# Second stage of an attention and two-layer expert kernel in two passes of four units, with partial sums in DRAM

## Chip, cores and metric

The kernel runs on one core of a Trainium2 chip. The metric is the device time of one execution in microseconds (us); the time before is the median of three runs, 1608.3 us (1608.15 to 1608.68).

## What is computed

Three layers follow each other. The first is an attention over 32 memory slots; its result (4608 tokens of 512) goes through a gated layer of width 1536, and that through a layer of width 2048.

```python
a = softmax(phi, over the sequence)            # 8 batches, 8 heads, 576 x 32
k_m, v_m = a^T k, a^T v                        # 32 x 64 for each head
x = softmax(q k_m^T / 8) v_m                   # 4608 x 512
x = (silu(x w_gate) * (x w_val)) w_out         # width 1536
out = elu(x w_in) w_out2                       # width 2048
```

All weights come as float64 and are turned into float32 parts on the chip.

## The kernel before

The hidden layer of 1536 is cut into twelve **units** of 128 (NU1 = 12), two units to a **pair**; a batch has 576 tokens, worked in two **halves** of HS = 288 columns. Every float32 product is made of three matmuls on rounded parts (high by high, high by low, low by high), so a unit's gate and val take 6 matmuls each (`up1`, tiles pg and pv) and its share of the output 4 x 3 (`down`).

- **Attention weights.** Since v_m has only 32 rows for each head, `vw` (L133) multiplies it into the gate and val weights of a pair: 16 short matmuls (pvw), then ACT and VectorE make the two parts (L143, L144). A unit's gate and val are then products of a vw tile and the attention probabilities `at`.
- **Stage 1** runs over the 8 batches with units 0 to 3 (UA = 4). Beside the matmuls of batch b stand the attention tasks of batches b + 1 and b + 2 and conversions of weights, dealt out by `tick`. The sum of the four units goes to DRAM as p1 (`down1`, L373), and `at` does too.
- **Stage 2** runs over the batches again with units 4 to 11. `load2` brings `at` back (tile at2); `load_p1` brings the partial sum of a half into the p1 tile, of which there is one buffer (L453). `down2` runs two units late (LAG = 2); with the last unit of a half it adds the four accumulators to p1 (L475) and stores the half as x1 (L476).
- **Stage 3** takes x1 in nine blocks of 512 tokens through 16 units (`unit3`, `down3`; tiles pu, g, e).
- **Conversion** of a weight tile (`load_w`, L86): a 512 KB load of float64 (wr, four buffers) on SP; ACT (L100); four VectorE instructions on the tiles wv and wc (L101, L102, L104, L105), the last of which reads wr and frees it; then, for tiles that are split, ACT (L107) and two GpSimd instructions (L108, L109), else one (L111). There are 68: 24 of w1g (four to a pair), 12 of w1o, 32 of w2 (two halves to each of 16 units).
- **What sets the order.** A scheduler orders each engine's instructions; L98 keeps a conversion behind the last h traced before it. Engines and SP's queue run in that order, and an instruction that waits holds those behind it.

Before the change, w1g of pairs 4 and 5 and w1o 7 to 11 are converted in the last batch of stage 1 (L411 to L413); 19 halves of w2 follow in stage 2, one in most halves and eight in the last batch (L518), and 13 in stage 3, one per unit (L526, L583).

Of the kernel before, what the change touches and what calls it, by code (L numbers as in the profile page):

```python
# [8 lines left out]
F32 = mybir.dt.float32  # L9
# [9 lines left out]
B, H, S, D, M = 8, 8, 576, 64, 32  # L19
NT = B * S  # L20
DM, F1, F2 = 512, 1536, 2048
KD = DM // 128
HS = S // 2
# [3 lines left out]
UA = 4  # L27
NCH = 5
NWA = 24
NWB = 16  # L30
NWE = 14
NWC = 10
NKV = 5
NQ = 3

# [2 lines left out]
def attention_moe_moe(ctx: ExitStack, tc: tile.TileContext, qT, phiT, kv, kv4, w1g, w1o, w2, out):  # L38
    nc = tc.nc
# [30 lines left out]

    at_d = [dram.tile([128, 2, 2, S], F32R, name=f"atd{b}") for b in range(B)]
    p1_d = [dram.tile([128, KD, S], F32, name=f"p1d{b}") for b in range(B)]
    x1_d = [dram.tile([128, KD, S], F32, name=f"x1d{b}") for b in range(B)]

    last = {}
# [43 lines left out]
    def load_wg(p, k, pool):  # L119
        load_w(WG, p, k, w1g[p, k], pool, False)  # L120

    def load_wo(u, pool):
        load_w(WO, u, 0, w1o[u], pool)
# [9 lines left out]
    def vw(b, p, pools):  # L133
        t = VW[b, p] = vx_p.tile([128, 2, 2, 512], F32R, tag="vx", name="vw")
        ps = [pool.tile([128, 512], F32, tag=tag, name="pvw") for pool, tag in pools]

        def head(j, g):
            r, c = slice(64 * g, 64 * g + 64), slice(32 * j, 32 * j + 32)
            return mm(ps[g][c], lhsT=Bs[b].vt[r, j, :], rhs=WG[p][j][r], start=True, stop=True)  # L139

        together([lambda j=j, g=g: head(j, g) for j in reversed(range(KD)) for g in (1, 0)])
        for g in range(2):
            act(out=t[:, 0, g, :], in_=ps[g], func=AF.Copy)  # L143
            tt(out=t[:, 1, g, :], in0=ps[g], in1=t[:, 0, g, :].bitcast(F32), op=ALU.subtract)  # L144
# [10 lines left out]
    def down(ps, w, hs, ms, start, stop):  # L155
        mm(ps, lhsT=w[0][:, ms], rhs=hs[0], start=start, stop=False)  # L156
        mm(ps, lhsT=w[1][:, ms], rhs=hs[0], start=False, stop=False)  # L157
        mm(ps, lhsT=w[0][:, ms], rhs=hs[1], start=False, stop=stop)  # L158
# [224 lines left out]
    def load2(b):  # L383
        at2[b] = av_p.tile([128, 2, 2, S], F32R, tag="at", name="at2")
        nc.sync.dma_start(out=at2[b].bitcast(F32), in_=at_d[b].bitcast(F32))


    def wg_tasks(p):
        return [lambda k=k: load_wg(p, k, wa_p) for k in range(KD)]

    prev = None
    for b in range(B):
        todo = []
# [14 lines left out]
            fr += [lambda u=u: load_wo(u, wb_p) for u in (4, 5, 6)]  # L408
        if b == B - 1:
            fr.append(lambda: load2(0))  # L410
            fr += wg_tasks(4) + [lambda: load_wo(7, wb_p), lambda: vw(0, 2, V2), lambda: load_wo(8, wb_p)]  # L411
            fr += wg_tasks(5) + [lambda: load_wo(9, wb_p), lambda: vw(0, 3, V2), lambda: load_wo(10, wb_p),
                                 lambda: load_wo(11, wb_p)]  # L413
        for i in range(max(len(bk), len(fr))):
            todo += fr[i:i + 1] + bk[i:i + 1]
        if b + 1 < B:
# [41 lines left out]
    def more_w2(pool, n=1):  # L458
        for _ in range(n):
            load_w2(*todo2.pop(0), pool)  # L460

    def load_p1(b, hf):
        t = p1_p.tile([128, KD, HS], F32, tag="p1", name="p1l")
        nc.sync.dma_start(out=t, in_=p1_d[b][:, :, HS * hf:HS * hf + HS])
        return t

    def down2(q):
        b, hf, u, hs, accs, p1 = q
        if u == UA:
            accs += [ps_acc.tile([128, HS], F32, tag=f"acc{m}", name=f"acc{m}") for m in range(KD)]  # L470
        for m in range(KD):
            down(accs[m], WO[u][0], hs, slice(128 * m, 128 * m + 128), u == UA, u == NU1 - 1)
        if u == NU1 - 1:
            for m in range(KD):
                tt(out=p1[:, m, :], in0=accs[m], in1=p1[:, m, :], op=ALU.add)  # L475
            nc.sync.dma_start(out=x1_d[b][:, :, HS * hf:HS * hf + HS], in_=p1)  # L476

    def load3(j):
        xt = []
# [14 lines left out]

    LAG = 2
    pend = []
    for p in (4, 5):
        vw(0, p, V2)
    w2q = [wa_p] * 4 + [we_p] * 7 + [wa_p] * 8
    vwq = []  # L500
    for b in range(B):
        for hf in range(2):
            p1 = load_p1(b, hf)
            accs = []
            if hf == 0 and b + 1 < B:
                load2(b + 1)
            for u in range(UA, NU1):
                s = gate1(b, u, at2[b], HS * hf, True)
                pend.append((b, hf, u, val1(b, u, at2[b], HS * hf, s, True), accs, p1))
                if len(pend) > LAG:  # L510
                    down2(pend.pop(0))
                if vwq:
                    vw(*vwq.pop(0), V2)
                if hf == 1 and u % 2 == 1 and b + 1 < B:
                    vwq.append((b + 1, u // 2))
                elif hf == 1 and u == 7 and b == B - 1:
                    nxt = load3(0)
                if u % 2 == 1 if b == B - 1 else u == 8 and len(w2q) > 8:  # L518
                    more_w2(w2q.pop(0))
# [105 lines left out]
```

## Time and profile before

| | us |
|---|---|
| median of three runs | 1608.3 |
| profiled execution: time | 1609.44 |
| profiled execution: span | 1607.6 |
| TensorE (PE) busy | 1533.4 |
| VectorE (DVE) busy | 988.0 |
| ScalarE (ACT) busy | 654.0 |
| GpSimd (POOL) busy | 166.2 |

The span is the time between the first and the last instruction of the profiled execution; its device time is 1.8 us longer. PE is the matmul engine, PEld its weight load, SP the engine that issues DMA transfers. Stage 1 lasts to about 361 us, stage 2 to about 811 us. Idle time of an engine counts only where the end of the kernel waits for it, so the views that matter are those by stretches and by waits.

### The profile page before, as it was taken

How to read it: one execution, taken by the hardware profiler on the slowest of the kernel's cores; microseconds unless marked ns; L12 is line 12 of the kernel's file. 1: busy time of each engine (PE TensorE's matmuls, PEld its weight loads, DVE VectorE, ACT ScalarE, POOL GpSimd, SP SyncE). 2: the span in 40 equal slices, each digit the busy share in tenths (PEclk: the TensorE clock that was granted, in tenths of full speed). 3: DMA queues.
4: the chain of work that ended last, by engine and by line, in shares of the span. 5: the costliest groups of instructions: out<-in, count | busy, mean ns of one | idle time of the engine just before them, and what ended most of it. 6: DMA issues, size and time to landing. Idle time of an engine off the chain costs nothing.

```text
span 1607.6 us, 24193 instructions
## 1 busy us (share of the span) xinstructions
PE 1533.4 (95%) x9816; PEld 1311.5 (82%) x9816; DVE 988.0 (61%) x1702; ACT 654.0 (41%) x1249; POOL 166.2 (10%) x119
## 2 busy tenths in 40 slices
PE   3599999979999999999998999999999999999998
PEld 2478789769999999999976788888888888888887
DVE  7997876795444454435889755555555555555554
ACT  3455444543333333333544433334343434343333
POOL 1400010241101011000435100000000000000000
PEclk7799999999999999999999999999999999999999
DMA  8887332452322232211522101001010101010000
GB/s 346 293 307 265 109 112 75 170 192 72 106 77 82 73 102 86 73 60 45 157 85 74 53 1 45 9 6 48 1 53 0 53 0 53 1 53 1 27 1 27
DMA packets 62961, 136.32 MB, mean 85 GB/s; under 512 B 6528, under 2 KB 37248, under 8 KB 60800
## 3 DMA queue, kind: packets, MB, share of 16 engines
q1 hardware_dynamic: 53632, 125.32, 22.7%
q10 hardware_dynamic: 9216, 9.44, 1.7%
q8 instruction: 77, 1.26, 0.3%
q14 instruction: 36, 0.29, 0.1%
HBM read 96.99 MB, written 37.75 MB: 84 GB/s over the span
## 4 chain that ended last, share of the span: by engine, by line
PE 81%; DVE 14%; DMA 2%; issue 2%; ACT 1%; SPq 0%; POOL 0%; ACTq 0%; DVEq 0%; POOLq 0%
PE acc L565 7%; PE acc L564 7%; PE acc L566 7%; PE pu L538 7%; PE pu L539 7%; PE pu L540 7%; PE acc L156 4%; PE acc L157 4%; PE acc L158 4%; PE pg L151 3%; PE pv L151 3%; PE pv L153 3%; PE pg L153 3%; PE pv L152 3%; PE pg L152 3%; PE pvw L139 3%
## 5 line engine op out<-in xcount | busy, mean ns | idle before, releaser
L538 PE MATMUL pu<-x1s,whi 128*128 128x512 f32 x576 | 224.7, 390 | 2.5 <-DVE g L554 2.5
L564 PE MATMUL acc<-whi,hh 128*128 128x512 f32 x576 | 224.5, 390 | 2.1 <-ACT hh L162 2.1
L566 PE MATMUL acc<-whi,hl 128*128 128x512 f32 x576 | 222.4, 390 | 3.3 <-DVE hl L164 3.3
L540 PE MATMUL pu<-x1s,wlo 128*128 128x512 f32 x576 | 224.8, 390 | 0.0
L539 PE MATMUL pu<-x1s,whi 128*128 128x512 f32 x576 | 224.7, 390 | 0.0
L565 PE MATMUL acc<-wlo,hh 128*128 128x512 f32 x576 | 224.2, 389 | 0.0
L553 DVE SCALAR_TENSOR_TENSOR g<-e,g 128x512 f32<-128x512 f32 x144 | 107.5, 747 | 157.5 <-ACT g L552 157.5
L162 ACT ACTIVATE hh<-g 128x512 fp32r<-128x512 f32 x144 | 91.0, 632 | 216.9 <-DVE g L554 216.9
L551 ACT ACTIVATE e<-g 128x512 f32<-128x512 f32 x144 | 90.8, 631 | 210.0 <-DVE g L550 210.0
L183 DVE SCALAR_TENSOR_TENSOR h<-s,pv 128x288 f32<-128x288 f32 x192 | 86.5, 451 | 140.8 <-PE pv L153 118.6
L164 DVE TENSOR_TENSOR hl<-g,hh 128x512 fp32r<-128x512 f32 x144 | 99.9, 694 | 88.3 <-ACT hh L162 88.2
L156 PE MATMUL acc<-hh,whi 128*128 128x288 f32 x512 | 151.0, 296 | 0.0
L157 PE MATMUL acc<-hh,wlo 128*128 128x288 f32 x512 | 150.6, 294 | 0.0
L158 PE MATMUL acc<-hl,whi 128*128 128x288 f32 x512 | 149.4, 295 | 0.0
L162 ACT ACTIVATE hh<-h 128x288 fp32r<-128x288 f32 x192 | 85.1, 443 | 138.9 <-DVE h L183 137.2
L164 DVE TENSOR_TENSOR hl<-h,hh 128x288 fp32r<-128x288 f32 x192 | 97.0, 505 | 63.0 <-ACT hh L162 62.8
L550 DVE TENSOR_SCALAR g<-pu 128x512 f32<-128x512 f32 x144 | 99.1, 689 | 55.2 <-PE pu L540 51.8
L566 PEld LDWEIGHTS acc<-whi,hl 128*128 128x128 f32 x576 | 108.0, 188 | 28.4 <-DVE hl L164 6.1
L151 PE MATMUL pg<-at,vw 128*128 128x288 f32 x384 | 119.4, 311 | 10.4 <-DVE vw L144 6.0
L564 PEld LDWEIGHTS acc<-whi,hh 128*128 128x128 f32 x576 | 108.3, 188 | 25.4 <-ACT hh L162 3.0
L538 PEld LDWEIGHTS pu<-x1s,whi 128*128 128x128 f32 x576 | 108.3, 188 | 25.3 <-DVE g L554 2.9
L539 PEld LDWEIGHTS pu<-x1s,whi 128*128 128x128 f32 x576 | 108.5, 188 | 22.6
(87 smaller groups left out, 3187.9 us busy)
## 6 DMA issues: line engine op xcount, KB each, us to landing
kvr<-kv SPq DMA_DIRECT2D x32, 512.0 KB, 7.9
wr<-w SPq DMA_DIRECT2D x32, 512.0 KB, 3.6
wr<-w1g SPq DMA_DIRECT2D x24, 512.0 KB, 4.9
qr<-qT SPq DMA_DIRECT2D x16, 576.0 KB, 5.9
atd<-at SPq DMA_DIRECT2D x8, 1152.0 KB, 5.3
p1d<-p ACTq DMA_DIRECT2D x64, 144.0 KB, 2.0
p1l<-p1d SPq DMA_DIRECT2D x16, 576.0 KB, 4.1
at<-atd SPq DMA_DIRECT2D x8, 1152.0 KB, 5.2
```

What stands on the lines that cost most here:

```text
L151: mm(ps, lhsT=wh, rhs=ah, start=g == 0, stop=False)
L156: mm(ps, lhsT=w[0][:, ms], rhs=hs[0], start=start, stop=False)
L157: mm(ps, lhsT=w[1][:, ms], rhs=hs[0], start=False, stop=False)
L158: mm(ps, lhsT=w[0][:, ms], rhs=hs[1], start=False, stop=stop)
L162: act(out=hh, in_=h, func=AF.Copy)
L164: tt(out=hl, in0=h, in1=hh.bitcast(F32), op=ALU.subtract)
L538: mm(ps, lhsT=wh[:, k, :], rhs=xh, start=k == 0, stop=False)
L539: mm(ps, lhsT=wh[:, k, :], rhs=xl, start=False, stop=False)
L540: mm(ps, lhsT=wl[:, k, :], rhs=xh, start=False, stop=k == KD - 1)
L564: mm(accs[c], lhsT=hs[0][:, cs], rhs=wh, start=u == 0, stop=False)
L565: mm(accs[c], lhsT=hs[0][:, cs], rhs=wl_, start=False, stop=False)
L566: mm(accs[c], lhsT=hs[1][:, cs], rhs=wh, start=False, stop=u == NU2 - 1)
```

## The change

Stage 2 runs over the batches twice. The first pass takes units 4 to 7, adds p1 and stores the result in a new DRAM buffer p2; the second takes units 8 to 11, adds p2 and stores x1. Of the conversions in the last batch of stage 1 only w1o 7 stays. The others and 22 halves of w2 are queued in `conv`, of which stage 2 takes one in each half, and two in each half of the last batch of the second pass; ten halves of w2 are left for stage 3. The vw of pairs 4 and 5 are made when the second pass comes to them.

```diff
-NWB = 16
-NWE = 14
-NWC = 10
+NWB = 8
+NWE = 20
+NWC = 12
...
+    p2_d = [dram.tile([128, KD, S], F32, name=f"p2d{b}") for b in range(B)]
...
-            fr += wg_tasks(4) + [lambda: load_wo(7, wb_p), lambda: vw(0, 2, V2), lambda: load_wo(8, wb_p)]
-            fr += wg_tasks(5) + [lambda: load_wo(9, wb_p), lambda: vw(0, 3, V2), lambda: load_wo(10, wb_p),
-                                 lambda: load_wo(11, wb_p)]
+            fr += [lambda: load_wo(7, wb_p), lambda: vw(0, 2, V2), lambda: vw(0, 3, V2)]
...
     def down2(q):
-        b, hf, u, hs, accs, p1 = q
-        if u == UA:
+        b, hf, u, hs, accs, p1, dst = q
+        first, last_u = u % UA == 0, u % UA == UA - 1
+        if first:
...
-            nc.sync.dma_start(out=x1_d[b][:, :, HS * hf:HS * hf + HS], in_=p1)
+            nc.sync.dma_start(out=dst[b][:, :, HS * hf:HS * hf + HS], in_=p1)
...
-    for p in (4, 5):
-        vw(0, p, V2)
-    w2q = [wa_p] * 4 + [we_p] * 7 + [wa_p] * 8
+
+    conv = [lambda p=p, k=k: load_wg(p, k, wa_p) for p in (4, 5) for k in range(KD)] + \
+        [lambda u=u: load_wo(u, wa_p) for u in range(2 * UA, NU1)] + \
+        [lambda pool=pool: more_w2(pool) for pool in [we_p] * 10 + [wa_p] * 4 + [wb_p] * 4 + [wa_p] * 4]
     vwq = []
...
+    for ps, (src, dst) in enumerate(((p1_d, p2_d), (p2_d, x1_d))):
+        for b in range(B):
+            nb, np_ = (b + 1, ps) if b + 1 < B else (0, ps + 1)
+            for hf in range(2):
+                p1 = load_p1(b, hf, src)
+                accs = []
+                if hf == 0 and np_ < 2:
+                    load2(nb)
+                for u in range(UA * (ps + 1), UA * (ps + 2)):
...
+                    if hf == 1 and u % 2 == 1 and np_ < 2:
+                        vwq.append((nb, u // 2 + UA // 2 * (np_ - ps)))
+                    elif hf == 1 and u == 9 and np_ == 2:
+                        nxt = load3(0)
+                    if u % (2 if np_ == 2 else 4) == 1:
+                        conv.pop(0)()
...
-    w2q = [wb_p] * 8 + [wc_p] * 5
+    w2q = [wa_p] * 4 + [wc_p] * 6
```

Lines of the changed kernel lie one further up to L383 of before (L101 becomes L102, L183 L184); L475, L476 and L464 become L472, L473 and L460.

On **VectorE in the last batch of stage 1** there stood before, among others, these twelve instructions in a row (wc and wv are a conversion's, h and hl a unit's):

```order
L144 TENSOR_TENSOR vw<-pvw,vw 128x512
L105 SCALAR_TENSOR_TENSOR wc<-wr,wc 128x512
L104 TENSOR_SCALAR wc<-wv 128x512
L144 TENSOR_TENSOR vw<-pvw,vw 128x512
L183 SCALAR_TENSOR_TENSOR h<-s,pv 128x288
L105 SCALAR_TENSOR_TENSOR wc<-wr,wc 128x512
L164 TENSOR_TENSOR hl<-h,hh 128x288
L101 TENSOR_SCALAR wc<-wv 128x512
L183 SCALAR_TENSOR_TENSOR h<-s,pv 128x288
L102 SCALAR_TENSOR_TENSOR wv<-wv,wc 128x512
L101 TENSOR_SCALAR wc<-wv 128x512
L104 TENSOR_SCALAR wc<-wv 128x512
```

In the changed kernel this follows between the same two vw tiles:

```order
L145 TENSOR_TENSOR vw<-pvw,vw 128x512 x2
L184 SCALAR_TENSOR_TENSOR h<-s,pv 128x288
L165 TENSOR_TENSOR hl<-h,hh 128x288
L184 SCALAR_TENSOR_TENSOR h<-s,pv 128x288
L165 TENSOR_TENSOR hl<-h,hh 128x288
L145 TENSOR_TENSOR vw<-pvw,vw 128x512 x2
```

The conversions between the two vw and behind them are gone; what is left there are the h and hl of two units.

On **VectorE at the end of a half of stage 2** (here the first) the four adds stood before between the h and hl of the unit that comes after:

```order
L183 SCALAR_TENSOR_TENSOR h<-s,pv 128x288
L475 TENSOR_TENSOR p1l<-acc_4616,p1l 128x288
L475 TENSOR_TENSOR p1l<-acc_4617,p1l 128x288
L164 TENSOR_TENSOR hl<-h,hh 128x288
L475 TENSOR_TENSOR p1l<-acc_4618,p1l 128x288
L475 TENSOR_TENSOR p1l<-acc_4619,p1l 128x288
```

Now the steps of a conversion stand among them:

```order
L184 SCALAR_TENSOR_TENSOR h<-s,pv 128x288
L102 TENSOR_SCALAR wc<-wv 128x512
L472 TENSOR_TENSOR p1l<-acc_4461,p1l 128x288
L472 TENSOR_TENSOR p1l<-acc_4462,p1l 128x288
L103 SCALAR_TENSOR_TENSOR wv<-wv,wc 128x512
L165 TENSOR_TENSOR hl<-h,hh 128x288
L472 TENSOR_TENSOR p1l<-acc_4463,p1l 128x288
L472 TENSOR_TENSOR p1l<-acc_4464,p1l 128x288
L105 TENSOR_SCALAR wc<-wv 128x512
L184 SCALAR_TENSOR_TENSOR h<-s,pv 128x288
L106 SCALAR_TENSOR_TENSOR wc<-wr,wc 128x512
```

L102 of the conversion moved ahead of the adds, L103 between them, L105 and L106 behind; in all 30 halves that are not in the last batch of the second pass it reads so or nearly so.

On **SP in stage 2**, around the stores of batch 2, a raw weight load (wr) stood before behind the load of p1, and the load of p1 right behind the store that frees its buffer:

```order
L88 DMA wr<-w 128x1024
L476 DMA x1d_125<-p1l 512x1x288
L464 DMA p1l<-p1d_117 128x4x288
L88 DMA wr<-w 128x1024
L385 DMA at_6472<-atd_111 128x2304
L476 DMA x1d_125<-p1l 512x1x288
L464 DMA p1l<-p1d_118 128x4x288
```

Now a raw weight load stands between that store and the load of p1:

```order
L460 DMA p1l<-p1d_117 128x4x288
L473 DMA p2d_125<-p1l 512x1x288
L89 DMA wr<-w1o 128x1024
L460 DMA p1l<-p1d_117 128x4x288
L386 DMA at_5382<-atd_111 128x2304
L473 DMA p2d_125<-p1l 512x1x288
L89 DMA wr<-w1o 128x1024
L460 DMA p1l<-p1d_118 128x4x288
```

The load of the next batch's at2 (L386) now follows the p1 load of each first half; the store of a first half comes behind it.

## Rows read from the trace of the kernel before

**Rows 1.** the page, busy us of each engine, share of the span, instructions.
```profile
PE 1533.4 (95%) x9816; PEld 1311.5 (82%) x9816; DVE 988.0 (61%) x1702; ACT 654.0 (41%) x1249; POOL 166.2 (10%) x119
```

**Rows 2.** busy us by stretches (then granted clock, DMA share, GB/s), a stage 2 batch.
```profile
451.06:506.78 55.72, 55.72 (x457) 51.73 (x463) 26.21 (x56) 20.16 (x44) 6.29 (x4) 1.00 0.26 84
```

**Rows 3.** the same view, last batch of stage 1 into stage 2.
```profile
315.30:367.29 51.99, 42.86 (x313) 35.88 (x312) 50.11 (x74) 26.20 (x56) 25.04 (x18) 0.93 0.58 194
```

**Rows 4.** groups of TensorE there: count, busy us, mean ns, idle before and what ended it.
```profile
L156 PE MATMUL pd<-hh,whi 128*128 128x288 f32 x48 | 14.5, 304 | 1.7 <-DVE vw L144 1.2 <-DVE h L183 0.4
...
L151 PE MATMUL pg<-at,vw 128*128 128x288 f32 x18 | 6.3, 348 | 5.7 <-DVE vw L144 5.7
...
L139 PE MATMUL pvw<-wg,vt 64*32 64x512 f32 x64 | 5.8, 630 | 1.5 <-ACT p L377 1.4 <-DVE h L183 0.2
L151 PE MATMUL pv<-at,vw 128*128 128x288 f32 x17 | 5.7, 337 | 0.2 <-DVE h L183 0.2
```

**Rows 5.** TensorE in order of time there: start, us, idle before and what ended it.
```profile
361.24 0.61 PE L151 MATMUL pg<-at,vw 128*128 128x288 f32 x1 [3.47 <-DVE vw L144]
```

**Rows 6.** the chain that ended last, in order of time: start, us, what.
```profile
356.31 3.50 DMA wr<-w
...
360.50 0.70 DVE vw L144
```

**Rows 7.** VectorE in order of time, adds of a half within a conversion.
```profile
757.32 0.42 DVE L101 TENSOR_SCALAR wc<-wv 128x512 int32<-128x512 int32 x1
757.66 0.81 DVE L475 TENSOR_TENSOR p1l<-acc,p1l 128x288 f32<-128x288 f32 x2
758.39 0.68 DVE L102 SCALAR_TENSOR_TENSOR wv<-wv,wc 128x512 int32<-128x512 int32 x1
...
759.36 0.81 DVE L475 TENSOR_TENSOR p1l<-acc,p1l 128x288 f32<-128x288 f32 x2
...
760.79 1.70 DVE L105 SCALAR_TENSOR_TENSOR wc<-wr,wc 128x512 f32<-128x512 uint32 x1
```

**Rows 8.** next matmul on the accumulators, in order of time; then busy time by stretches.
```profile
760.59 0.29 PE L156 MATMUL acc<-hh,whi 128*128 128x288 f32 x1
...
760.00:780.00 20.00, 20.00 (x153) 20.00 (x152) 14.67 (x28) 8.56 (x20) 9.81 (x7) 1.00 0.42 139
```

**Rows 9.** SP's DMA issues in order of time, same place.
```profile
760.20 0.54 SPq L476 DMA_DIRECT2D x1d<-p1l  x1
762.57 0.33 SPq L88 DMA_DIRECT2D wr<-w  x1
763.50 0.54 SPq L464 DMA_DIRECT2D p1l<-p1d  x1
```

**Rows 10.** groups of TensorE from 830 to 900 us, head of stage 3.
```profile
L564 PE MATMUL acc<-whi,hh 128*128 128x512 f32 x50 | 19.7, 395 | 2.1 <-ACT hh L162 2.1
L566 PE MATMUL acc<-whi,hl 128*128 128x512 f32 x51 | 19.5, 405 | 3.3 <-DVE hl L164 3.3
```

**Rows 11.** p1 loads (L464) issued before 300 us, from 300 to 750, from 750.
```profile
DMA to landing us min/median/max: 8.8/8.8/8.8
...
DMA to landing us min/median/max: 4.0/4.1/4.2
...
DMA to landing us min/median/max: 5.2/5.7/6.1
```

**Rows 12.** stage 2 to 3: the chain that ended last, then TensorE in order of time.
```profile
811.19 3.30 DMA x1d<-p1l
...
819.52 0.50 PE L538 MATMUL pu<-x1s,whi 128*128 128x512 f32 x1 [2.47 <-DVE g L554]
```

**Rows 13.** busy time by stretches, 100 us of stage 3.
```profile
1010.00:1110.00 100.00, 100.00 (x443) 82.81 (x442) 54.99 (x82) 37.94 (x61) 0.00 (x0) 1.00 0.07 22
```

**Rows 14.** GpSimd in order of time, first step of two conversions in stage 3.
```profile
886.94 1.74 POOL L108 TENSOR_TENSOR wv<-wv,whi 128x512 f32<-128x512 f32 x1 [2.69 <-DVE wc L104]
...
893.08 1.73 POOL L108 TENSOR_TENSOR wv<-wv,whi 128x512 f32<-128x512 f32 x1 [2.70 <-DVE wc L104]
```

More of the change, by code (lines that the diff above doesn't have):

```diff
@@ L460, in more_w2, with load_p1 @@
             load_w2(*todo2.pop(0), pool)
-    def load_p1(b, hf):
+    def load_p1(b, hf, src):
         t = p1_p.tile([128, KD, HS], F32, tag="p1", name="p1l")
-        nc.sync.dma_start(out=t, in_=p1_d[b][:, :, HS * hf:HS * hf + HS])
+        nc.sync.dma_start(out=t, in_=src[b][:, :, HS * hf:HS * hf + HS])
         return t
     def down2(q):
-        b, hf, u, hs, accs, p1 = q
-        if u == UA:
+        b, hf, u, hs, accs, p1, dst = q
+        first, last_u = u % UA == 0, u % UA == UA - 1
+        if first:
             accs += [ps_acc.tile([128, HS], F32, tag=f"acc{m}", name=f"acc{m}") for m in range(KD)]
         for m in range(KD):
-            down(accs[m], WO[u][0], hs, slice(128 * m, 128 * m + 128), u == UA, u == NU1 - 1)
-        if u == NU1 - 1:
+            down(accs[m], WO[u][0], hs, slice(128 * m, 128 * m + 128), first, last_u)
+        if last_u:
             for m in range(KD):
                 tt(out=p1[:, m, :], in0=accs[m], in1=p1[:, m, :], op=ALU.add)
-            nc.sync.dma_start(out=x1_d[b][:, :, HS * hf:HS * hf + HS], in_=p1)
+            nc.sync.dma_start(out=dst[b][:, :, HS * hf:HS * hf + HS], in_=p1)
     def load3(j):
@@ L496, in attention_moe_moe @@
     pend = []
-    for p in (4, 5):
-        vw(0, p, V2)
-    w2q = [wa_p] * 4 + [we_p] * 7 + [wa_p] * 8
+    conv = [lambda p=p, k=k: load_wg(p, k, wa_p) for p in (4, 5) for k in range(KD)] + \
+        [lambda u=u: load_wo(u, wa_p) for u in range(2 * UA, NU1)] + \
+        [lambda pool=pool: more_w2(pool) for pool in [we_p] * 10 + [wa_p] * 4 + [wb_p] * 4 + [wa_p] * 4]
     vwq = []
[L501 to L519, printed above, removed]
+    for ps, (src, dst) in enumerate(((p1_d, p2_d), (p2_d, x1_d))):
[7 more added lines that the diff above has]
+                for u in range(UA * (ps + 1), UA * (ps + 2)):
+                    s = gate1(b, u, at2[b], HS * hf, True)
+                    pend.append((b, hf, u, val1(b, u, at2[b], HS * hf, s, True), accs, p1, dst))
+                    if len(pend) > LAG:
+                        down2(pend.pop(0))
+                    if vwq:
+                        vw(*vwq.pop(0), V2)
+                    if hf == 1 and u % 2 == 1 and np_ < 2:
[4 more added lines that the diff above has]
+                        conv.pop(0)()
     for q in pend:
```

2 lines of the change are left out of this document (removed).

## Prediction, made before the changed kernel ran

> **What bounds the kernel now.** The busy times of the whole run come first [rows 1]: TensorE works 1533.4 of 1607.6 us and VectorE 988.0, so a gain has to come out of the 74 us in which TensorE stands idle, or out of stretches with a lowered clock. The busy time by stretches shows where those lie. From 451 to 507 us, one whole batch of the second stage, TensorE is busy all 55.72 us and VectorE 26.21 [rows 2]: nothing is to be had there. Two stretches are left on which the change bears. The first is the last batch of stage 1 and the first units of stage 2, 315.30 to 367.29 us: TensorE 42.86 of 51.99 us at a mean granted clock of 0.93, VectorE 50.11 of 51.99 [rows 3]. The second is the head of stage 3, where matmuls wait 2.1 us for hh and 3.3 us for hl [rows 10].
>
> How much the first stretch loses is counted by work. Its groups hold 3x48 matmuls of pd, 3x18 of pg and 3x17 of pv, 249 in all, and 64 short ones of pvw, four vw tiles of 16 [rows 4]. A clean batch takes 55.72 us for 16 units of 24 matmuls and four vw [rows 2]. With 1.09 us for one vw, the matmul stands at (55.72 - 4.4) / 384 = 0.134 us. So the stretch holds 249 x 0.134 + 4 x 1.09 = 37.7 us of work and loses 51.99 - 37.7 = **14.3 us**. Of this 9.1 us is recorded idle time (51.99 - 42.86). The longest single wait, 3.47 us, is that of the first gate matmul of stage 2 at 361.24 us for a vw tile [rows 5]; the chain of waits leads from there back through vw to a raw weight load [rows 6], the start of a conversion. The clock of 0.93, 7% of 52 us, is another 3.6 us: TensorE had been idle just before.
>
> **The change, part by part.**
>
> *Conversions leave the tail of stage 1.* Of the 13 conversions of the last batch (eight w1g, w1o 7 to 11) one stays, w1o 7. The order of VectorE shows the rest gone and h and hl back to back. The two vw of pairs 4 and 5 move too, but their 16 matmuls each are done later, so that they count on neither side. What stays: a thirteenth of the loss, 1.1 us, and the 0.4 us for which pd waits for the last h (inside the 1.7 us of L156, [rows 4]). Gain 14.3 - 1.5 = **12.8 us**; not below the recorded idle less that, 9.1 - 1.5 = 7.6, nor above 14.3.
>
> *Two passes.* The matmuls are the same in kind and number. Per half batch (288 columns, four units) the change doubles the adds of L475, the stores of a half and the loads of a half, reloads at2 once more per batch, and puts one conversion in each half: 34 in stage 2 for 19. A batch of before keeps VectorE busy 26.21 us, with 56 instructions: 32 of h and hl, 8 of vw, 8 adds, two conversions of four [rows 2]. To that come 8 adds at 0.81 / 2 us and two conversions, L101 and L104 at 0.42 each, L102 0.68, L105 1.70, 3.2 us [rows 7]: (26.21 + 3.2 + 6.4) / 4 = 9.0 of the 13.9 us of a half (55.72 / 4). So VectorE has room, and the question is only order: the adds free the accumulators, and now stand between the steps of a conversion. That very order occurs once in the trace of before, at 757 us: h, L101, two adds, L102, hl, two adds, L104, h, L105 [rows 7]. The adds were through at 759.36 + 0.81 = 760.17. The next group on the accumulators began at 760.59, and from 760 to 780 us TensorE was busy 20.00 of 20 us, with VectorE at 14.67 and conversions every other unit, twice as dense as the change makes them [rows 8]. I take nothing for the order itself and 1.0 us in all over the 32 halves for chance meetings; from 0 up to the price of the second rival.
>
> *The p1 tile.* There is one buffer. A half's load waits for the store of the half before, and that for its adds; a raw weight load now stands on SP between store and load, waiting for L105. The trace has this as well [rows 9]: first add 757.66, store issued 760.20, raw load 762.57, p1 load 763.50, so 5.84 us from the first add to the load's issue. The load then lands in 5.2 us, where loads with nothing in front landed in 4.0 to 4.2 [rows 11]; together 11.0 us. The next adds come four units on: 4 x 24 x 0.134 = 12.8 us in the halves without a vw between, 15.0 in the others. So the load is there 1.8 us early and costs **0** as long as it lands within 7.0 us. In every other half an at2 load (1152 KB) is issued behind it, which no row shows in this place. The Trainium skill (DMA: Bandwidth & Descriptors, Queues, rings and completion order) has each DMA engine take descriptors in the order of its ring; by that, the raw load in front counts (1.1 us here, which agrees) and at2 behind does not, and the sum stays as it is; without the rule the half with at2 would be the one to fail. This is the first rival.
>
> *Out of stage 2 into stage 3.* By the order of TensorE, 18 matmuls of pu stood ahead of the last one on acc before, and 22 do now. The first g of stage 3 hangs on that last matmul: it waits for the store of the last half, 3.30 us, since its buffer lies where p1 lay, and TensorE then stands 2.47 us [rows 12]. The same holds after the change. Four matmuls at 100 / 443 us [rows 13] make the last acc later by **0.9 us**; between 0 and 1.8, twice that.
>
> *Head of stage 3.* One conversion per unit, 13 before, 10 now, since 22 of the 32 w2 halves instead of 19 are done by then. Two of them in a row stand 893.08 - 886.94 = 6.14 us apart [rows 14], against 24 x 100 / 443 = 5.42 us for a unit without one [rows 13]. Three fewer give 3 x 0.72 = **2.2 us**; between 0 (the lead of TensorE hides it) and the 5.4 us of waiting for hh and hl there [rows 10].
>
> Sum: -12.8 + 1.0 + 0 + 0.9 - 2.2 = -13.1 us. The profiled run had a span of 1607.6 and a time of 1609.4 us, 1.8 more; its time lies 1.1 above the median of the three runs. So span 1594.5, time 1596.3, median **1595.2 us**.
>
> **The rivals.**
>
> *The p1 chain becomes the bound (slower).* Price: two chains per batch, 2 x (5.84 + L) for a landing time L, against 2 x 13.93 us of matmul. It binds once L is above 8.1 us in both halves. At 8.8 us, the longest p1 landing of the trace (the first, among the traffic of stage 1, [rows 11]), a batch takes 29.3 for 27.9 us; over 16 batches 22.7 us, less some 2 us of lead, is 1595.2 + 20.7 = 1616 us. It makes the kernel slower than before by more than 0.2% from L = 8.6 us on. For it: one buffer, a raw load in front, at2 behind. Against it: 15 of 16 landings lay at 4.0 to 6.1 us.
>
> *A conversion in stage 2 costs what it cost in stage 1.* 14.3 us for 13 is 1.1 us each; 15 more of them in stage 2 eat 16.5 us, for the 1.0 in the sum: 1595.2 + 15.5 = 1610.7 us. Against it: rows 2 and 8, in which TensorE runs through conversions without a gap. For it: L105 took 1.70 us while POOL worked, where L102, as large, took 0.68 [rows 7]. The Trainium skill (SBUF — State Buffer, Who interferes with whom) says that a VectorE instruction with two inputs in SBUF and a GpSimd instruction that reads SBUF block each other for a whole instruction. The 1.70 us agree; by that rule each added conversion would hold VectorE up by about 1 us, 15 us in all, which the 4.9 us to spare in a half take up, so that it would cost something only where h or an add stands right behind.
>
> *The tail of stage 1 doesn't get shorter,* because something other than the conversions holds it. Then only 2.2 - 1.9 = 0.3 us are left: 1608 us. Against it: VectorE is busy 96% of that stretch [rows 3], and the chain in front of its longest wait is a conversion's [rows 6].
>
> **How the numbers follow.** My forecast has 0.81, with a range of its own from 1590 to 1601 (its terms at their bounds, not all at once). The p1 chain 0.07, costly conversions 0.06, an unshortened tail 0.06. A measurement can tell 0.2% from no change, 3.2 us: 1605.1 to 1611.5. Faster: the forecast but for its worst corner, 0.81, and 0.03 for milder forms of the rivals, 0.84. Same: the second and third rival for the most part, 0.09. Slower: the chain, and the second rival at its worst, 0.07. The range, to hold 8 in 10: 1589.5, with 5 us more from the bounds of the first and last term, to 1603, which takes in half-strength rivals.
>
> **What would show it.** Right: in the profile after, the last batch of stage 1 has VectorE far below full and no clock drop at its end, and the first gate of stage 2 stands near 350 us, not 361 (315.3 + 231 x 0.134 + 2 x 1.09 + 1.5); a batch of both passes takes twice 27.9 us; p1 loads land within 7 us and no add waits for one; conversions in stage 3 end at the tenth unit. Wrong: DVE waiting for DMA p1l at the adds (first rival), gaps in TensorE at each half boundary that end with an add (second), idle TensorE before stage 2 with VectorE idle too (third).

## The result, and the profile after

The changed kernel takes 1596.4 us in the median (1593.1 to 1598.4, four runs), the kernel before 1608.5 (1608.2 to 1611.9, four runs, three of them those named at the start). The ratio is 0.9918 with a 95% interval of 0.9896 to 0.994: 12.1 us less, where 13.1 were forecast (1595.2 us, 1589.5 to 1603).

The profiled execution of the changed kernel has a span of 1591.3 us and a time of 1593.1, the fastest of the four. TensorE works nearly as long as before [rows 1], VectorE 31 us more (mostly the adds of the second pass, 64 more of 0.45 us). From the page, busy time and instructions of each engine, and what went through memory (96.99 MB read and 37.75 written before):

```profile
PE 1524.7 (96%) x9816; PEld 1308.1 (82%) x9816; DVE 1018.6 (64%) x1766; ACT 650.9 (41%) x1249; POOL 156.0 (10%) x119
...
HBM read 115.87 MB, written 47.19 MB: 102 GB/s over the span
```

The same view by stretches as [rows 2, 3], of the tail of stage 1 and of a batch of each pass (after the stretch: busy time and count of TensorE, its weight loads, VectorE, ScalarE and GpSimd; granted clock; DMA share; GB/s):

```profile
313.00:345.82 32.82, 32.82 (x263) 30.81 (x262) 11.71 (x24) 15.06 (x34) 3.12 (x2) 1.00 0.35 122
438.00:465.88 27.88, 27.88 (x226) 25.88 (x225) 17.34 (x36) 9.81 (x23) 3.50 (x3) 1.00 0.48 162
633.00:660.88 27.88, 27.88 (x226) 25.88 (x225) 18.73 (x36) 10.91 (x24) 5.25 (x5) 1.00 0.50 166
```

TensorE has no gap left in the tail and VectorE is busy 11.71 of 32.82 us, where it was busy 50.11 of 51.99. The first gate matmul of stage 2 begins at 345.82, without a wait, where it began at 361.24 after a wait of 3.47 [rows 5]. A batch of one pass takes 27.88 us with TensorE busy throughout and VectorE for 17.34 to 18.73 of them.

**Equal work.** Both kernels issue the same number of matmuls. Leave out the short ones of pvw, number the other 9048 in order, and take the start of the n-th in a kernel's trace less that in the changed kernel's trace: this lag is how much later the kernel is at that point of its work. Where it changes, time is lost or won. All kernels of the experiments stand in one table (us; in the second row "before" and "one_pass" (one_pass_no_conv) have done two vw tiles more, 2 x 1.1 us; in the third their order of work differs too much to compare):

```
n (at, in the changed kernel)      before  tail_back  one_pass  conv_twice  p1_load_again
2293 (313.08, tail of stage 1)      2.30     3.98       2.00      0.99        4.97
2557 (350.56, stage 2 has begun)   19.21    16.18       5.25      0.99        4.97
5293 (746.99, last batch but one)    -      16.12        -        4.52       11.79
5631 (797.91, last acc is through) 16.71    16.12       2.75      8.58       12.16
5711 (823.78, stage 3 runs)        13.37    15.88      -0.61     15.16       13.50
5991 (892.32, head is over)        16.29    16.03       2.32     16.40       14.62
9048 (1585.24, the last)           16.29    16.03       2.32     16.39       14.62

n                                  g_off_p1  p1_two  three_later  g_off_p1_two  spaced  off_two_spaced  after_again
2293                                 4.81     2.33      4.46         4.15        2.13       2.44           5.16
2557                                 4.81     2.33      4.46         4.15        2.13       2.44           5.16
5293                                 4.81     2.33      4.46         4.15        2.13       2.45           5.16
5631                                 4.81     2.33      4.43         4.15        2.13       2.44           5.16
5711                                -1.62     2.33      1.92        -2.50        0.25      -4.72           3.82
5991                                 1.11     2.38      4.83         0.21       -4.83      -7.72           4.90
9048                                 1.11     2.38      4.83         0.21       -4.83      -7.72           4.90
```

Read for the kernel before, the 16.3 us between the two traces are: 2.3 at the start (nothing of the change: the code is the same there); 19.21 - 2.30 - 2.2 = **14.7** in the tail; 19.21 - 2.2 - 16.71 = 0.3 given back in all of stage 2; 16.71 - 13.37 = **3.3** given back on the way into stage 3; 16.29 - 13.37 = **2.9** won at its head. After that both run alike.

In stage 2 the adds of a half stand between the steps of a conversion in just the order that [rows 7] showed once. VectorE in order of time:

```profile
403.83 0.42 DVE L102 TENSOR_SCALAR wc<-wv 128x512 int32<-128x512 int32 x1
404.17 0.81 DVE L472 TENSOR_TENSOR p1l<-acc,p1l 128x288 f32<-128x288 f32 x2
404.90 0.68 DVE L103 SCALAR_TENSOR_TENSOR wv<-wv,wc 128x512 int32<-128x512 int32 x1
405.50 0.45 DVE L165 TENSOR_TENSOR hl<-h,hh 128x288 fp32r<-128x288 f32 x1
405.87 0.81 DVE L472 TENSOR_TENSOR p1l<-acc,p1l 128x288 f32<-128x288 f32 x2
406.60 0.41 DVE L105 TENSOR_SCALAR wc<-wv 128x512 int32<-128x512 int32 x1
406.93 0.44 DVE L184 SCALAR_TENSOR_TENSOR h<-s,pv 128x288 f32<-128x288 f32 x1
407.30 0.68 DVE L106 SCALAR_TENSOR_TENSOR wc<-wr,wc 128x512 f32<-128x512 uint32 x1
```

The chain of the p1 tile, SP's DMA issues from the store of one half to the next load but one, and the loads and stores of both passes (count, KB, median us to landing):

```profile
406.70 0.54 SPq L473 DMA_DIRECT2D p2d<-p1l  x1
408.05 0.33 SPq L89 DMA_DIRECT2D wr<-w1o  x1
410.18 0.54 SPq L460 DMA_DIRECT2D p1l<-p1d  x1
...
422.94 0.54 SPq L460 DMA_DIRECT2D p1l<-p1d  x1
423.95 0.33 SPq L386 DMA_DIRECT2D at<-atd  x1
```

```profile
p1l<-p1d SPq DMA_DIRECT2D x15, 576.0 KB, 4.6
```

```profile
p1l<-p2d SPq DMA_DIRECT2D x16, 576.0 KB, 5.4
```

From the first add (404.17) to the load's issue (410.18) pass 6.01 us; the next issue stands 12.76 us on, so the loads ahead of such a tight interval may take 12.76 - 6.01 = 6.7 us. The loads take 4.6 and 5.4 in the median of the two passes, and up to the last batch none ahead of a tight interval takes more than 5.8. Only one add of stage 2 waits for a load, for 1.4 us, in the last half. The chain of waits on the way into stage 3, in order of time, then TensorE, then busy time:

```profile
786.03 3.50 DMA x1d<-p1l
...
789.55 5.47 DMA p1l<-p2d
...
795.14 1.56 DVE p1l L472 x4
...
796.72 3.28 DMA x1d<-p1l
```

```profile
805.07 0.80 PE L538 MATMUL pu<-x1s,whi 128*128 128x512 f32 x1 [4.74 <-DVE g L554]
```

```profile
800.00:810.00 10.00, 5.26 (x14) 3.86 (x13) 8.16 (x15) 5.70 (x9) 0.82 (x1) 0.70 0.00 0
820.00:830.00 10.00, 10.00 (x46) 8.29 (x45) 10.00 (x15) 5.50 (x9) 5.86 (x4) 1.00 0.29 86
840.00:850.00 10.00, 8.74 (x39) 7.05 (x38) 9.96 (x13) 4.33 (x7) 5.30 (x5) 1.00 0.13 50
850.00:860.00 10.00, 7.37 (x30) 5.14 (x30) 9.86 (x15) 4.98 (x9) 4.86 (x3) 1.00 0.00 0
```

The kernel before, behind its own stop:

```profile
820.00:830.00 10.00, 10.00 (x39) 8.05 (x38) 9.96 (x15) 5.54 (x10) 4.64 (x4) 0.83 0.25 86
```

The last store of x1d is issued at 796.72, because the adds ahead of it waited for the p1 load that was issued at 789.55. The first g waits for this store, and TensorE stands 4.74 us (2.47 in [rows 12]). The granted clock is 0.70 in the mean from 800 to 810 us and 0.96 in the next 10: 6.8 us at half clock, where the kernel before has 3.4 (0.83 in its row). At the head of stage 3 VectorE is busy 10.00 of 10 us from 820 to 830, 9.96 and 9.86 from 840 to 860, and TensorE has gaps from 840 to 860.

### The profile page after: what moved, and what is told of

The parts are those of the page before. It is cut to its first block, busy times and chain, and to the rows that moved or that the text cites. A ratio compares the mean times of both kernels' runs of the same rounds, so it can differ in the third digit from the quotient of the medians.

```text
span 1591.3 us, 24347 instructions
## 1 busy us (share of the span) xinstructions
PE 1524.7 (96%) x9816; PEld 1308.1 (82%) x9816; DVE 1018.6 (64%) x1766; ACT 650.9 (41%) x1249; POOL 156.0 (10%) x119
## 4 chain that ended last, share of the span: by engine, by line
PE 83%; DVE 12%; DMA 2%; issue 1%; ACT 1%; SPq 0%; ACTq 0%; DVEq 0%
PE acc L565 8%; PE acc L566 8%; PE acc L564 8%; PE pu L540 8%; PE pu L539 8%; PE pu L538 8%; PE acc L157 4%; PE acc L159 4%; PE acc L158 4%; PE pg L152 3%; PE pv L152 3%; PE pv L153 3%; PE pv L154 3%; PE pg L154 3%; PE pg L153 3%; PE pvw L140 3%
## 5 line engine op out<-in xcount | busy, mean ns | idle before, releaser
L184 DVE SCALAR_TENSOR_TENSOR h<-s,pv 128x288 f32<-128x288 f32 x192 | 86.3, 450 | 108.2 <-PE pv L154 97.9
L165 DVE TENSOR_TENSOR hl<-h,hh 128x288 fp32r<-128x288 f32 x192 | 105.5, 549 | 53.8 <-ACT hh L163 53.8
L540 PEld LDWEIGHTS pu<-x1s,wlo 128*128 128x128 f32 x576 | 108.6, 189 | 22.3
```

What stands on the lines that cost most here:

```text
L165: tt(out=hl, in0=h, in1=hh.bitcast(F32), op=ALU.subtract)
L540: mm(ps, lhsT=wl[:, k, :], rhs=xh, start=False, stop=k == KD - 1)
```

## Experiments

Theory: the gain is the tail's alone, since the conversions there leave VectorE's queue; the second pass costs nothing beside TensorE; what is left over comes from the way into stage 3. Rivals: the passes or another order make the gain; conversions cost the same in stage 2; the p1 chain takes some.

**tail_back: two passes, conversions back in the tail.**

```diff
-            fr += [lambda: load_wo(7, wb_p), lambda: vw(0, 2, V2), lambda: vw(0, 3, V2)]
+            fr += [lambda k=k: load_wg(4, k, wa_p) for k in range(KD)]
+            fr += [lambda: load_wo(7, wb_p), lambda: vw(0, 2, V2), lambda: load_wo(8, wb_p)]
+            fr += [lambda k=k: load_wg(5, k, wa_p) for k in range(KD)]
+            fr += [lambda: load_wo(9, wb_p), lambda: vw(0, 3, V2), lambda: load_wo(10, wb_p),
+                   lambda: load_wo(11, wb_p)]
...
-    conv = [lambda p=p, k=k: load_wg(p, k, wa_p) for p in (4, 5) for k in range(KD)] + \
-        [lambda u=u: load_wo(u, wa_p) for u in range(2 * UA, NU1)] + \
+    conv = [lambda: None] * 12 + \
...
```

The pools that hold the converted tiles have other sizes, too.

> The changed kernel with its two passes, but with the twelve conversions (w1g of pairs 4 and 5, w1o 8 to 11) back in the last batch of stage 1; stage 2 converts only its 22 w2 halves, at the same places as in the changed kernel. My theory: the gain is that of the tail alone, 14.7 us between the two traces (TensorE's lead at equal work grows from 2.3 us to 19.2 us there, of which two vw tiles, 2.2 us, are work done later). So this kernel is back at the time of before: 1609 to 1611 us, VectorE over 90% busy in the last batch of stage 1 and the first gate matmul of stage 2 some 11 to 13 us later than in the changed kernel. Rival, the gain is made by the passes themselves or by the order in stage 2: the time stays near 1596 us.

Measured 1608.5 us, just below the forecast, ratio to before 0.999 (0.9981 to 0.9999): the gain is gone. By the table it loses 16.18 - 3.98 = 12.2 us in the tail and nothing more than the changed kernel afterwards. Its tail by stretches, to be set beside the row of 313.00:

```profile
317.00:349.82 32.82, 29.20 (x217) 26.30 (x216) 31.54 (x49) 17.29 (x37) 14.66 (x10) 0.95 0.52 179
```

VectorE is full again (31.54 of 32.82) and the clock is down to 0.95. The loss is 2.5 us smaller than before's 14.7; the two vw tiles of pairs 4 and 5, which stood at the end of that stretch before, are not in it. They explain 1.05 us of the difference (next experiment); the other 1.4 stay open. The forecast of the first gate can't be read: this kernel's order has gates of stage 2 between the last pd matmuls.

**one_pass_no_conv: the kernel before, without the twelve conversions.**

```diff
-            fr += wg_tasks(4) + [lambda: load_wo(7, wb_p), lambda: vw(0, 2, V2), lambda: load_wo(8, wb_p)]
-            fr += wg_tasks(5) + [lambda: load_wo(9, wb_p), lambda: vw(0, 3, V2), lambda: load_wo(10, wb_p),
-                                 lambda: load_wo(11, wb_p)]
+            fr += [lambda: load_wo(7, wb_p), lambda: vw(0, 2, V2), lambda: vw(0, 3, V2)]
...
+    WG[4:6], WO[8:12] = WG[2:4], WO[4:8]
```

> The kernel before, with one pass, without the twelve conversions in the last batch of stage 1: stage 2 takes the weights of pairs 2 and 3 for pairs 4 and 5 and those of units 4 to 7 for units 8 to 11, so the values differ, the work of TensorE is the same. My theory: 1608.5 - 14.7 = 1594 us (1592 to 1596), the tail runs without a drop of the clock. Rival, something other than the conversions holds the tail: 1605 to 1609 us.

Measured 1597.2 us, ratio 0.9919 (0.9903 to 0.9934), a little above the forecast and the same as the changed kernel's 0.9918. So leaving those conversions out altogether is worth no more than the two passes are: what the second pass adds is hidden. Up to the first gate of stage 2 its tail is that of the changed kernel:

```profile
315.00:347.82 32.82, 32.82 (x262) 30.73 (x261) 11.71 (x24) 15.05 (x34) 3.12 (x2) 1.00 0.34 122
```

Behind that row it makes the two vw tiles of pairs 4 and 5, and there it loses 5.25 - 2.00 - 2.2 = 1.05 us beyond their work, without the twelve conversions. So of the 14.7 us at most 13.7 are the conversions' (12.2 by tail_back), and 1.05 come from the place of these two vw tiles, which the change moved too.

Like the kernel before it wins 3.4 us on the way into stage 3 against the changed kernel and loses 2.9 at the head.

**conv_twice: each conversion of stage 2 computed twice.**

```diff
+    times = [1]
...
-        v = wt_p.tile([128, 512], F32, tag="wv", name="wv")
...
+        for _ in range(times[0]):
+            v = wt_p.tile([128, 512], F32, tag="wv", name="wv")
...
+                        times[0] = 2
                         conv.pop(0)()
+                        times[0] = 1
```

> The changed kernel, each of the 34 conversions of stage 2 computed twice from the same raw tile (no transfer more). My theory: a conversion in stage 2 lies beside TensorE's work; VectorE goes from about 9.0 to between 11.2 and 12.2 us of the 13.9 us of a half, and nothing is lost in the steady part: 1596 to 1602 us, the upper end for the last batch, where conversions stand in every other unit. Rival, a conversion costs in stage 2 what it cost in stage 1, 1.1 us: 34 x 1.1 = 37 us more, 1634 us.

Measured 1609.3 us, ratio 0.9998 (0.9988 to 1.0007): some 13 us more than the changed kernel, more than the forecast and far less than the rival. The table says where. Over the first pass the lag stays at 0.9 to 1.0 us, though VectorE now works up to 24.30 of 27.88 us; in the second pass 3.5 us go (0.99 to 4.52); in the last batch and on the way into stage 3 10.6 (4.52 to 15.16), a part of it by the clock (0.81 in the third row). By stretches, a batch of each pass and the way into stage 3, and TensorE's longest wait there:

```profile
438.00:465.88 27.88, 27.88 (x226) 25.88 (x225) 21.12 (x44) 11.92 (x25) 6.82 (x5) 1.00 0.47 165
633.00:660.88 27.88, 27.88 (x226) 25.88 (x226) 24.30 (x45) 13.25 (x28) 11.46 (x8) 1.00 0.48 166
800.00:820.00 20.00, 7.86 (x39) 6.10 (x37) 16.02 (x24) 7.77 (x12) 10.42 (x7) 0.81 0.31 106
```

```profile
PE pu L542 <- DVE g L558: 11.4, 1, 11.4
```

So a conversion more in each half costs nothing in the first pass and 0.25 us in the second (3.5 / 14). A conversion in the last half is on the path: the last adds, which everything of stage 3 waits for, stand behind it on VectorE.

**p1_load_again: a longer p1 chain.**

```diff
+        nc.sync.dma_start(out=t[:, 0:2], in_=src[b][:, 0:2, HS * hf:HS * hf + HS])
         nc.sync.dma_start(out=t, in_=src[b][:, :, HS * hf:HS * hf + HS])
```

> The changed kernel, half of each p1 tile loaded once more ahead of the whole load, into the same tile, so that the second load waits for the first: the chain add, store, raw load, p1 load is longer by one landing of about 3.5 us. My theory: the chain of the changed kernel, 6.0 us and a landing of 4.1 to 6.1, leaves 0.6 to 2.6 us to spare against the 12.7 us of the tight halves; with 3.5 us more two chains take 27.2 to 31 us against 27.9 us of work per batch, so the batches whose loads land in over 4.5 us (about 11 of 16) lose some 2 us each: 1610 to 1630 us, and VectorE waits for the p1 load at the adds. Rival, the load is so well hidden that 3.5 us don't show: 1596 to 1598 us.

Measured 1607.7 us, ratio 0.9989 (0.9976 to 1.0002), below the forecast. What VectorE waited for between 350 and 800 us (us in total, times, longest):

```profile
DVE p1l L473 <- DMA p1l<-p1d: 14.2, 9, 3.2
DVE p1l L473 <- DMA p1l<-p2d: 6.5, 4, 2.1
```

Thirteen adds wait 20.7 us for a load, and the table shows 12.16 - 4.97 = 7.2 us lost, from the 3400th matmul on. The chain became longer by less than was forecast: the half load lands in 3.7 us in the median, but the whole one behind it in 4.1 instead of 5.4, 7.8 together. At 7.8 us adds wait in the tight halves, and the others make most of it up. What TensorE itself waits for meanwhile is mostly a vw tile that stands behind the late adds on VectorE (six waits, 3.8 us), and only once an add (0.4 us). Another 2.5 us go on the way into stage 3 and at its head (12.16 to 14.62). The mechanism of the first rival is real, and the changed kernel's longest landing ahead of a tight interval, 5.8 us, is 0.9 from the 6.7 where it begins.

**g_off_p1: g away from p1's place.**

```diff
-NWC = 12
+NWC = 8
...
-    w2q = [wa_p] * 4 + [wc_p] * 6
...
     t3_p = ctx.enter_context(tc.tile_pool(name="t3", bufs=2, side="right"))
+    wd_p = ctx.enter_context(tc.tile_pool(name="wd", bufs=4, side="right"))
+    w2q = [wa_p] * 4 + [wc_p] * 4 + [wd_p] * 2
```

> The changed kernel with another order of the tiles of stage 3: four of the twelve tiles of wc lie behind those of g, e, hh and hl, so that g no longer lies where p1 lay and doesn't wait for the last store of x1d. My theory: the wait of g for that store, 3.4 us, and the half clock that follows TensorE's 4.7 us of idle time are what the way from stage 2 to stage 3 lost beyond my sum (3.3 us more than before, where 0.9 were forecast); without the wait TensorE stands about 1 us there and stage 3 begins 4 to 7 us earlier: ratio to the kernel before 0.9875 to 0.9895. Rival, TensorE's stop there is that of the first g chain itself (VectorE with adds and conversions, ScalarE), and the store is hidden behind it: no more than 1 us, ratio 0.991 to 0.992.

Measured 1592.7 us, ratio 0.9889 (0.9873 to 0.9904), as forecast. TensorE's only stop between 600 and 812 us, and the head of stage 3 by stretches:

```profile
806.12 0.50 PE L539 MATMUL pu<-x1s,whi 128*128 128x512 f32 x1 [0.97 <-DVE g L555]
```

```profile
800.00:810.00 10.00, 9.03 (x40) 7.17 (x39) 8.15 (x17) 6.26 (x9) 1.67 (x2) 1.00 0.30 109
820.00:830.00 10.00, 9.12 (x41) 7.13 (x40) 10.00 (x13) 5.19 (x10) 5.78 (x4) 1.00 0.18 64
```

The clock no longer drops, and 4.81 + 1.62 = 6.4 us are won on the way into stage 3. But 2.7 of them go again at the head (-1.62 to 1.11), where VectorE is full and TensorE now has gaps from 820 on.

**p1_two: two p1 tiles.**

```diff
-    p1_p = st_p1.enter_context(tc.tile_pool(name="p1", bufs=1, side="right"))
+    p1_p = st_p1.enter_context(tc.tile_pool(name="p1", bufs=2, side="right"))
```

> The changed kernel with two p1 tiles, so that a half's load no longer waits for the store of the half before. My theory: the chain of the p1 tile binds nowhere but in the last half, where the adds wait 1.4 us for the load: 0 to 3 us faster than the changed kernel, all of it behind the last add of stage 2, ratio 0.990 to 0.992; in the steady part TensorE's lead over the changed kernel doesn't change by 0.3 us. Rival, the chain takes a little at each half: a lead that grows from batch to batch, 5 us or more.

Measured 1596.1 us, ratio 0.9911 (0.9897 to 0.9926). The lag is 2.33 us from the 2293rd to the 5711th matmul: the chain takes nothing anywhere in the steady part. Not even the 1.4 us of the last half came back, and VectorE shows why:

```profile
796.39 1.55 DVE L472 TENSOR_TENSOR p1l<-acc,p1l 128x288 f32<-128x288 f32 x4 [0.23 <-PE acc L159]
802.66 1.29 DVE L550 TENSOR_SCALAR g<-pu 128x512 f32<-128x512 f32 x2 [4.71 <-DMA x1d<-p1l]
```

```profile
791.15 5.38 SPq L89 DMA_DIRECT2D wr<-w  x2
```

```profile
797.98 4.49 DMA x1d<-p1l
```

The adds no longer wait for a load (0.23 us for TensorE). But SP, which doesn't wait for a p1 tile any more, issues two raw loads just ahead of the store (797.98), and the store lands in 4.49 us for 3.28; g waits 4.71 for 3.43. The Trainium skill (DMA: Bandwidth & Descriptors, Queues, rings and completion order) has an engine take descriptors in the order of its ring, so that a store behind two loads comes later; these rows agree.

**three_later: three conversions from the end of stage 2 to stage 3.**

```diff
-        [lambda pool=pool: more_w2(pool) for pool in [we_p] * 10 + [wa_p] * 4 + [wb_p] * 4 + [wa_p] * 4]
+        [lambda pool=pool: more_w2(pool) for pool in [we_p] * 10 + [wa_p] * 4 + [wb_p] * 4 + [wa_p]]
...
-                    if u % (2 if np_ == 2 else 4) == 1:
+                    if conv and u % (2 if np_ == 2 else 4) == 1:
...
-    w2q = [wa_p] * 4 + [wc_p] * 6
+    w2q = [wa_p] * 7 + [wc_p] * 6
```

> The changed kernel with the last three conversions of stage 2 in the first units of stage 3 (13 there, as in the kernel before, instead of 10). My theory: by the traces three conversions at the head of stage 3 cost 2.9 us (TensorE's lead over the kernel before grows from 13.4 to 16.3 us between the units 2 and 13): 2 to 3 us slower there, less 0 to 3 us because the last batch of stage 2 has one conversion instead of four; ratio 0.990 to 0.994. Rival, the conversions at the head are hidden, and the 2.9 us come from the order of the units: no loss at the head.

Measured 1597.9 us, ratio 0.9921 (0.9908 to 0.9933). By the table 4.83 - 1.92 = 2.9 us are lost at the head, as forecast, and 4.43 - 1.92 = 2.5 won ahead of it (up to 1.3 of that may be the half clock, 3.4 us long here and 6.8 in the changed kernel's trace, as under after_again). But the 2.9 us are not the conversions' alone. What is won just ahead of the head goes in part again at the head (1.1 of 1.3 us in after_again), and the head has a stretch of half clock that the changed kernel's trace lacks, 3.4 us, worth up to 1.7:

```profile
850.00:860.00 10.00, 8.16 (x29) 5.99 (x28) 9.87 (x12) 4.67 (x8) 6.86 (x5) 0.85 0.41 150
```

So 0.97 us for each of the three conversions is an upper figure. By the table the whole edit costs 4.83 - 4.46 = 0.4 us.

**g_off_p1_two: both.** The two diffs above together.

> Both: g apart from p1, and two p1 tiles. My theory: the first chain of g starts when the adds are done, and these no longer wait for a load: 5 to 9 us faster than the changed kernel, ratio 0.986 to 0.989, with TensorE's idle time before stage 3 under 1 us and no half clock there. Rival, as for the two alone: VectorE's conversions hold the first g, and less than 2 us are gained.

Measured 1590.3 us, ratio 0.988 (0.9864 to 0.9895). 4.15 + 2.50 = 6.7 us won before stage 3, 2.7 lost at its head. The second p1 tile adds 0.2 us by the table.

**spaced, off_two_spaced: stage 3's conversions in two of three units.**

```diff
-            if w2q:
+            if w2q and u % 3 < 2:
                 more_w2(w2q.pop(0))
```

> The changed kernel with the ten conversions of stage 3 in two of three units (0, 1, 3, 4, 6, 7, 9, 10, 12, 13) instead of in each of the units 0 to 9. My theory: a unit of 5.44 us with a conversion asks more of VectorE than it has (VectorE is busy 10.00 of 10 us from 820 to 860 us in the changed kernel), which is why the head loses about 5 us there; with a free unit in between VectorE catches up, and 3 to 5 us of it come back: ratio 0.9885 to 0.990. Rival, a conversion costs the same 0.7 to 0.9 us in whichever unit it stands (through order, not through load): no gain, 0.991 to 0.992.

> The kernel with g apart from p1 and two p1 tiles, and with the spacing of the conversions of stage 3. My theory: the former gained 6.7 us on the way into stage 3 and gave 2.8 back at its head, where VectorE was full; spacing brings back 4 to 7 us: ratio 0.984 to 0.9855. Rival, no gain from the spacing: 0.988.

Measured 1588.3 us, ratio 0.9873 (0.9856 to 0.989), and 1585.6 us, 0.9853 (0.9838 to 0.9868): the first is faster than forecast, the last as forecast and the fastest kernel of this study. The head by stretches, of the changed kernel with spacing alone, to be read beside the rows of 840.00 and 850.00 above, and all that TensorE waited for from 780 to 890 us in the kernel with all three edits:

```profile
840.00:850.00 10.00, 10.00 (x46) 8.29 (x45) 7.30 (x11) 4.52 (x9) 3.35 (x2) 1.00 0.15 54
850.00:860.00 10.00, 10.00 (x46) 8.28 (x45) 9.22 (x15) 5.49 (x9) 4.72 (x3) 1.00 0.00 0
```

```profile
PE pu L541 <- POOL wlo L110: 0.7, 1, 0.7
PE pu L539 <- DVE g L555: 0.2, 1, 0.2
```

With a free unit between two conversions VectorE falls to 7.30 and 9.22 of 10 us and TensorE's gaps are gone: 0.25 + 4.83 = 5.1 us. The changed kernel takes 883.26 - 823.78 = 59.5 us for 240 matmuls there, at the steady rate of stage 3 (9.07 us for 40) 54.4 us, so spacing gives back all of the 5.1 that the head lost. Another 2.13 - 0.25 = 1.9 us are won on the way into stage 3, up to 1.3 of it by the half clock, which is 3.4 us long in this trace.

**after_again: the changed kernel once more.**

> The changed kernel once more, beside the others, for its spread. My theory: its runs differ by the stretches of half clock in the first 210 us alone, 0 to 5 us by the traces, and from there to the end two traces of it agree within 0.1 us but for the clock behind TensorE's stop before stage 3: 1595 to 1598 us, ratio 0.991 to 0.9925. Rival, the runs differ in the second stage (by transfers that land at other times): a lead that changes from batch to batch.

Measured 1595.3 us (1593.2 to 1598.0), ratio 0.9909 (0.9891 to 0.9928). Its trace lies 5.16 us behind the first one of the same kernel, all of it from the first 213 us; from there to the 5631st matmul the two agree to 0.01 us. On the way into stage 3 it loses 1.3 us less (3.4 us at half clock for 6.8, behind a stop of 4.48 us for 4.74), and 1.1 of that go again at the head.

## Why the prediction was right, step by step

*Tail of stage 1: right, a little too small.* 12.8 us forecast, 14.7 measured, just over the bound of 14.3. The mechanism was the one named, and tail_back and one_pass_no_conv show it: the conversions in VectorE's queue, the matmuls waiting behind them and the lowered clock. They make 12.2 to 13.7 us of it; 1.05 are the place of the two vw tiles of pairs 4 and 5, which the sum counted on neither side. The sum kept 1.5 us (a thirteenth for w1o 7 and pd's wait for the last h); TensorE is busy 32.82 of 32.82 us there, so nothing of that stays. The first gate was forecast near 350 from 315.30, that is 34.7 us on; it came 345.82 - 313.0 = 32.8 on.

*Two passes: right.* 1.0 us forecast, 0.3 measured. VectorE was forecast at 9.0 us per half and is busy 8.7 to 9.4 (half of 17.34 and 18.73). The second rival, 1.1 us per conversion, is refuted by conv_twice: of its 34 additional conversions the 16 of the first pass cost nothing, the next 14 cost 3.5 us, where the rival asks for 15; only the four of the last batch are dear. The rule of the Trainium skill (SBUF — State Buffer, Who interferes with whom) was right about the duration, 1.70 us in [rows 7] for 0.68; in the changed kernel 22 of the 32 L106 from 350 to 780 us take 1.7 us, each beside a GpSimd instruction, and the others 0.7. An instruction that long cost TensorE nothing outside the last batch, since VectorE has the time to spare in a half.

*The p1 chain: right for the steady part.* 6.01 us to the load's issue (5.84 forecast), landings of 4.1 to 6.1 us, no wait before the last batch, and p1_two wins nothing. An at2 load behind it doesn't delay it: from 382 to 745 us the 13 loads with one issued behind them land in 4.1 to 6.1 us, the 14 others in 4.1 to 5.8. That is the ring order of the Trainium skill (DMA: Bandwidth & Descriptors, Queues, rings and completion order), and the trace agrees with it.

The prediction put the binding point at 8.1 us of landing in both halves, 7.0 in the tight ones; p1_load_again, at 7.8 in the median, which lies between, loses 7.2 us over the 16 batches, 0.45 each. Missed: in the last half the chain did bind, by 1.4 us. No units follow there: where they wait for no load, the last adds begin 11.3 us after the first add of the half before (796.39 - 785.1, in p1_two) and not 12.8. And the adds of the half before have subtractions of x1 between them on VectorE, so that the load is issued 6.9 us after the first of them (782.66 to 789.55) and not 6.0, and lands after 12.4.

*Way into stage 3: the step that was mis-sized.* 0.9 us forecast for four more pu matmuls ahead of the last acc (18 before, 22 now, as forecast), 3.3 measured. The prediction took the wait for the last store and the clock behind it as given. Both grew. TensorE's stop is 4.74 - 2.47 = 2.3 us longer, close to the 0.9 forecast and the 1.4 us that the last adds wait for the p1 load. The other 1.1 us go with the clock, at half for 6.8 us instead of 3.4. That length isn't the change's: in after_again the same kernel has 3.4 us, the add waits 1.13 us, the stop is 2.0 us longer than before, and by the table just 2.0 us are lost here ((16.71 - 5.16) - (13.37 - 3.82)). g_off_p1 shows the place, and what the wait costs in all: without it 6.4 us come back. That the late load alone makes the stop longer isn't shown by a run, since in p1_two, where the adds don't wait for it, the store lands later.

*Head of stage 3: right.* 2.2 us forecast for three conversions fewer, 2.9 measured with the first trace and 1.8 with the second ((16.29 - 4.90) - (13.37 - 3.82)); three_later, which puts the three back, loses 2.9 there, not all by the conversions. That VectorE's load is the cause is shown by spaced: the same ten conversions further apart, and the gaps are gone. Not foreseen: the two last terms aren't independent. VectorE is full at the head, so a part of what is won or lost just ahead of it is taken up there (2.7 of 6.4 us in g_off_p1, 1.1 of 1.3 in after_again).

*The sum.* -14.7 + 0.3 + 3.3 - 2.9 = -14.0 us, where -13.1 were forecast: the tail and the second pass came out 2.6 us better, the way into stage 3 2.4 worse, the head 0.7 better. That the sum is off by 0.9 us alone is in part luck: errors of 3.3 and 2.4 us stand against each other. The two traces differ by 2.3 us more, from the start. The medians differ by 12.1 us in the first comparison and by 1609.6 - 1595.3 = 14.3 in the last. In two comparisons between them the kernel before took 1610.2 (25 runs) and 1611.1 us (nine).

## What to carry to other kernels

When a stage is bound by one engine and its neighbour by another, work that has slack to wait can be moved to where the second engine is idle, even at the price of another pass through memory: here 28 MB more traffic (163.1 for 134.7) and 64 more adds cost 0.3 us. Look then at the seams, not at the steady part: a conversion, a load or a store that costs nothing in the middle of a stage is on the path in its last half, and two of the three seams here hung on a choice of place (a tile over another's, a conversion in each unit instead of in two of three). Compare traces by equal work, start of the n-th matmul against start of the n-th: it puts each microsecond at its place, and separates the start from what the change did.

## What the runs showed of the hardware

The thirteen traces run the same instructions up to some 260 us, and yet stand 0 to 5.2 us apart at 313 us; afterwards all that share an order agree to a few hundredths up to the way into stage 3. The difference is in stretches of half clock that come in some executions and not in others. One such place, by stretches, before, changed kernel, and changed kernel once more:

```profile
190.00:199.50 9.50, 8.01 (x80) 5.62 (x79) 9.50 (x24) 4.08 (x9) 0.00 (x0) 1.00 0.33 109
199.50:206.40 6.90, 6.90 (x32) 5.04 (x29) 4.99 (x8) 3.18 (x7) 2.55 (x2) 0.51 0.52 161
```

```profile
190.00:199.50 9.50, 8.02 (x81) 5.49 (x84) 9.50 (x24) 4.08 (x9) 0.00 (x0) 1.00 0.27 97
199.50:206.40 6.90, 6.03 (x45) 4.98 (x38) 5.57 (x10) 4.04 (x8) 2.57 (x2) 1.00 0.59 174
```

```profile
202.50:209.30 6.80, 6.80 (x33) 5.14 (x30) 4.77 (x7) 3.31 (x7) 2.56 (x2) 0.50 0.51 165
```

In all three TensorE had stood for 1.5 us at about 197 us (200 in the last), waiting for an s of VectorE, after much the same work (8.01 and 8.02 of 9.5 us in the first two). In two of them 6.8 us at 1.2 GHz follow, with 32 and 33 matmuls in the stretch; in the other it stays at 2.4 GHz and does 45. Six of the thirteen traces have this stretch. Here it cost 1.8 us (the lag of the kernel before grows from 0.43 to 2.26 us across it), and such stretches are, in the traces, what sets runs of one kernel up to 5 us apart: the lag of after_again grows by 1.6, 1.5 and 1.9 us across its stretches at 80, 127 and 203 us. Which executions get one stays open: nothing was found in the traces ahead of it that tells them apart.
